# A causal convolution and a gated projection on one core: convolution units moved between the column and the row products

## The chip, the core and the metric

The kernel runs on one core of a Trainium2 chip. The core has a matrix engine (TensorE, PE in the profile, with its weight loads shown apart as PEld), three engines for elementwise work (VectorE as DVE, ScalarE as ACT, GpSimd as POOL) and SyncE (SP), which here only issues DMA transfers. Each engine takes its instructions in the order of the program; between engines, semaphores hold an instruction until its inputs are there and its output buffer is free. TensorE writes its results to PSUM, of which this kernel has eight banks of 128 x 512 fp32: two for the gate of chunk 1, one for the gate of chunk 2 and five shared by everything else.

The metric is the device time of one execution in microseconds (us), here as the median over several runs.

## The reference

x has 8 sequences of 4224 positions and 192 features, 8 heads of 24. First each head is convolved with 7 causal taps, the softmax of 7 weights. On that result x works a gated layer: a causal convolution of 5 taps for each feature gives a gate through a sigmoid, x is projected by a 192 x 192 matrix, multiplied by the gate, and projected again.

```python
w = softmax(weight)                                   # 8 heads x 7
x = einsum('hk,bskhg->bshg', w, windows(x, 7))        # causal, per head
gate_pre = sum(conv_w[k] * shifted(x, k) for k in range(5))
gate = 1 / (1 + exp(-gate_pre))
out = (gate * (x @ w_val)) @ w_out
```

## The kernel before

The features lie on the partitions and the positions along the free dimension. 192 features don't fit in 128 partitions, so two streams of four sequences each are worked together: for each position, "chunk 1" holds 128 features of both streams (a tile of 128 x 2 x m), and "chunk 2" holds the last 64 features of both streams in the halves of one tile (128 x m). In the code the index 0 or 1 of a gate stands for chunk 1 or chunk 2; in the products q = 0 and 1 are the two streams of chunk 1 and q = 2 is chunk 2. To keep the word free, the steps of the main loop are called chunks n in the text below, and "chunk-1 taps" and "chunk-2 taps" name the taps of the gate for the two tiles, whose PSUM tiles are called pa and pb in the profile.

There are 36 chunks n, of up to m = 502 positions (304 and 302 in the first two, 448 in the next six, 502 from 8 to 31, 448 to 456 and 232 in the last four). They belong to 14 groups, and each group's convolved x comes out of the first stage, as follows.

- **Convolution units** (`conv_unit`, line 312). A unit is four windows of the 7-tap convolution, each a product of a window of x (weights on PE) with a band matrix (`band`), in fp32; the profile counts two matmuls for each. The result (tile pc) is copied by ScalarE to tile e (line 321). When a head is complete, `scatter` sends it with DMAs (line 348) into x1 and x2 of the group, and `load_x` issues the next loads of x (line 160); both go through SP's queue, for the first groups partly through POOL's. There are 114 units. `conv(k)` issues the next k of them, and the list `todo` says how many belong to each chunk n: 3, 6, 3, 5, 5, 4, 3, 3 in chunks 0 to 7, then 4, 3, 3 over and over in 8 to 25, 2 each in 26 to 31, none after that. They are for a group that is needed two groups later.
- **Gates**. `gate_open` (line 382) is a ScalarE instruction that starts the gate's sum in PSUM with the first tap; `gate_taps` (line 389) adds the other four on VectorE; `gate_close` (line 402) is ScalarE's sigmoid from PSUM to SBUF (g1 and g2). pa and pb have one buffer each, so a gate is opened only after the one before it is closed, and the next taps begin only when it is open.
- **Products in split precision**. A product in fp32 is done as three products of rounded parts, high and low: `split` and `split_gated1`, `split_gated2` make the parts, the high one by a ScalarE cast (lines 410, 418), the low one by a POOL subtraction (lines 411, 419).
- **The two projections**, "v" (x times w_val, of chunk n) and "o" (the gated product times w_out, of chunk n - 1). Each has four groups on PE: `diagonal` (line 445, chunk 2 to chunk 2, full array), `main` (line 455, chunk 1 to chunk 1, full array, three matmuls for each stream), `columns` (line 483, chunk 1 to chunk 2, 64 columns of the array for each stream) and `rows` (line 468, chunk 2 to chunk 1, 64 rows of the array for each stream).
- **Ends**. `gated(n, q)` (line 502) multiplies "v" with the gate on VectorE, out of PSUM; `project(n, q)` (line 518) copies "o" out of PSUM on ScalarE, and after q = 1 the output DMA is issued on SP (line 523).

Every engine's order is that of the code (`manual_schedule`). The five shared banks (pool `ps`) go round: `pc`, "v" and "o" tiles take a bank when their first matmul comes, and give it back when their last reader is done, which is `gated` for "v", `project` for "o" and the copy of line 321 for a unit. A tile's first matmul waits for the reader that gave its bank back. The main loop stands at the end of the function.

Of the kernel before, what the change touches and what calls it, by code (L numbers as in the profile page):

```python
# [99 lines left out]
def kernel(  # L100
# [197 lines left out]
    def conv_unit(u):  # L298
        g, q, ws = units[u]
        n = NJS[g]  # L300
        if u == first_unit[g]:
            x1s[g] = xp.tile([128, 2 * XB], F32, tag="x1", name=f"x1_{g}")
            x2s[g] = xp.tile([128, XC], F32, tag="x2", name=f"x2_{g}")
        if ws[0] == (0, 0):
            es[g, q] = ep.tile([M, 4 * NMAX * WIN], F32, tag="e", name=f"e_{g}_{q}")
        e = es[g, q]
        pc = ps.tile([128, 512], F32, tag="p", name=f"pc_{u}")
        for k, (hi, j) in enumerate(ws):
            h = QUADS[q][hi]
            i, at = home[g, h]  # L310
            c = (at * n + j) * M
            nc.tensor.matmul(  # L312
                pc[:M, k * WIN : (k + 1) * WIN],
                lhsT=xtiles[i][:, c : c + M],
                rhs=band[:, 4 * q + hi, :],
                start=True,
                stop=True,
            )
        a = (ws[0][0] * n + ws[0][1]) * WIN
        w = len(ws) * WIN  # L320
        nc.scalar.copy(e[:, a : a + w], pc[:M, :w])  # L321
        done = [hi for hi, j in ws if j == n - 1]
        for hi in done:
            h = QUADS[q][hi]
            i, at = home[g, h]
            last = at == len(loads[i][1]) - 1
            if last and g >= BY_POOL:
                load_x(allowed(i))
            scatter(g, h, e[:, hi * n * WIN : (hi + 1) * n * WIN])
            if last and g < BY_POOL:  # L330
                load_x(allowed(i))
# [31 lines left out]
    def views(n, k=KG - 1):  # L363
        g, o, m = STEPS[n]
        b = second(NJS[g])
        x1v = x1s[g][:, : 2 * b].rearrange("p (a t) -> p a t", a=2)
        return x1v[:, :, o + k : o + k + m], x2s[g][:, o + k : o + k + m]
# [5 lines left out]
    def gate_open(n, i):  # L373
        if n >= N:
            return
        m = STEPS[n][2]
        if i == 0:
            acc = ps_g.tile([128, 2, 512], F32, tag="pa", name=f"pa_{n}")[:, :, :m]
        else:
            acc = ps_h.tile([128, 512], F32, tag="pb", name=f"pb_{n}")[:, :m]  # L380
        accs[n, i] = acc
        nc.scalar.mul(acc, views(n, 0)[i], cwt[:, i, 0:1])  # L382

    def gate_taps(n, i, k0=1, k1=KG):
        if n >= N:
            return
        acc = accs[n, i]
        for k in range(k0, k1):
            nc.vector.scalar_tensor_tensor(  # L389
                out=acc, in0=views(n, k)[i], scalar=cwt[:, i, k : k + 1],  # L390
                in1=acc, op0=ALU.mult, op1=ALU.add,
            )

    def gate_close(n, i):
        if n >= N:
            return
        m = STEPS[n][2]
        if i == 0:
            dst = g1s[n] = gp.tile([128, 2, MB], F32, tag="g1", name=f"g1_{n}")[:, :, :m]
        else:  # L400
            dst = g2s[n] = gp.tile([128, MB], F32, tag="g2", name=f"g2_{n}")[:, :m]
        nc.scalar.activation(dst, accs.pop((n, i)), AF.Sigmoid)  # L402
# [21 lines left out]
    def bank(what, n, q):  # L424
        t = ps.tile([128, 512], F32, tag="p", name=f"{what}_{n}_{q}")[:, : STEPS[n][2]]
        banks[what, n, q] = t
        return t

    def operands(what, n):
        return (w_val, *xs[n, 1], *xs[n, 2]) if what == "v" else (w_out, *pr[n, 1], *pr[n, 2])  # L430

    def parts(w, h, l):
        return (w.h, h), (w.l, h), (w.h, l)

    def ok(n):
        return 0 <= n < N

    def diagonal(what, n):
        if not ok(n):
            return  # L440
        acc = bank(what, n, 2)
        w, _, _, h2, l2 = operands(what, n)
        r = slice(W22, W22 + 128)
        for i, (a, b) in enumerate(parts(w, h2, l2)):
            nc.tensor.matmul(acc, lhsT=a[:, r], rhs=b, start=(i == 0), stop=False)  # L445

    def main(what, n, q):
        if not ok(n):
            return
        fresh = (what, n, q) not in banks  # L450
        acc = bank(what, n, q) if fresh else banks[what, n, q]
        w, h, l, _, _ = operands(what, n)
        r = slice(W11, W11 + 128)
        for i, (a, b) in enumerate(parts(w, h, l)):
            nc.tensor.matmul(  # L455
                acc, lhsT=a[:, r], rhs=b[:, q], start=(fresh and i == 0), stop=(not fresh and i == 2)
            )

    def rows(what, n):
        if not ok(n):  # L460
            return
        fresh = (what, n, 0) not in banks
        two = [bank(what, n, q) if fresh else banks[what, n, q] for q in range(2)]
        w, _, _, h2, l2 = operands(what, n)
        r = slice(W21, W21 + 128)
        for i, (a, b) in enumerate(parts(w, h2, l2)):
            for acc, p in zip(two, HALVES):
                nc.tensor.matmul(  # L468
                    acc, lhsT=a[p, r], rhs=b[p], start=(fresh and i == 0), stop=(not fresh and i == 2)
                )  # L470

    def columns(what, n):
        if not ok(n):
            return
        m = STEPS[n][2]
        acc = banks[what, n, 2]
        w = w_val if what == "v" else w_out
        x = views(n)[0] if what == "v" else g1s[n]
        cuts = [m * i // 4 for i in range(5)]
        for i in range(4):  # L480
            c = slice(cuts[i], cuts[i + 1])
            for q, p in enumerate(HALVES):
                nc.tensor.matmul(  # L483
                    acc[p, c], lhsT=w.f[:, W12 : W12 + 64], rhs=x[:, q, c],
                    start=False, stop=(i == 3),
                )

    def split(n):
        if n >= N:
            return  # L490
        x1, x2 = views(n)
        if n == 0:
            xs[n, 2] = split2(sp, "x", n, x2)
        xs[n, 1] = split1(sp, "x", n, x1)
        if n > 0:
            xs[n, 2] = split2(sp, "x", n, x2)

    def gated(n, q):
        if not ok(n):
            return  # L500
        v = g1s[n][:, q] if q < 2 else g2s[n]
        nc.vector.tensor_tensor(out=v, in0=banks.pop(("v", n, q)), in1=v, op=ALU.mult)  # L502

    def split_gated1(n):
        if ok(n):
            pr[n, 1] = split1(pp, "p", n, g1s[n])

    def split_gated2(n):
        if ok(n):
            pr[n, 2] = split2(pp, "p", n, g2s[n])  # L510

    def project(n, q):
        if not ok(n):
            return
        m = STEPS[n][2]
        if n not in ots:
            ots[n] = op.tile([128, 3 * MB], F32, tag="ot", name=f"ot_{n}")
        nc.scalar.copy(ots[n][:, q * m : (q + 1) * m], banks.pop(("o", n, q)))  # L518
        o = 3 * sum(s[2] for s in STEPS[:n])
        if n == LAST:  # L520
            nc.sync.dma_start(out[:, o + q * m : o + (q + 1) * m], ots[n][:, q * m : (q + 1) * m])
        elif q == 1:
            nc.sync.dma_start(out[:, o : o + 3 * m], ots[n][:, : 3 * m])
# [9 lines left out]
    def conv(k):  # L533
        for _ in range(k):
            if done[0] < len(units):
                conv_unit(done[0])
                done[0] += 1

    todo = [0] * (N + 1)
# [31 lines left out]
    for n in range(N + 1):  # L571
        diagonal("v", n)
        gate_taps(n + 1, 0, 1, 3)
        split(n + 1)
        diagonal("o", n - 1)
        main("v", n, 0)
        main("v", n, 1)
        gate_taps(n + 1, 0, 3, KG)
        columns("v", n)
        gated(n, 2)  # L580
        gate_close(n + 1, 0)
        gate_open(n + 2, 0)
        columns("o", n - 1)
        split_gated2(n)
        project(n - 1, 2)
        rows("v", n)
        gated(n, 0)
        gated(n, 1)
        rows("o", n - 1)
        split_gated1(n)  # L590
        main("o", n - 1, 0)
        gate_taps(n + 1, 1)
        project(n - 1, 0)
        main("o", n - 1, 1)
        project(n - 1, 1)
        conv(todo[n])
        gate_close(n + 1, 1)
        gate_open(n + 2, 1)

# [89 lines left out]
```

## Time and profile before

| | |
|---|---|
| median of 3 runs | 393.77 us (392.7 to 394.51) |
| the profiled execution, its own time | 391.79 us |
| its span | 390.0 us |
| its granted TensorE clock | 0.99 of full speed |
| PE, DVE, ACT, POOL busy | 377.6, 343.5, 323.7, 254.6 us |

All views come from that one profiled execution. A row of the timeline begins with its start in us from the start of the span, and its length; then follow engine, line, operation, output and inputs, shapes and count, and in brackets the idle time of the engine just before it with what ended it. Neighbouring rows of one kind are merged, so that a row of "x4" covers four instructions. Instructions of VectorE and ScalarE that follow each other overlap by a little in such rows, so the distance from start to start is less than the length. A row of the chain of waits has a start, a length and what was on the chain. In the view of waits a row names an engine with its tile and line, what it waited for, the total in us, how often and the longest. "Issue" there is idle time for which no event is seen.

### The profile page before, as it was taken

The numbers are of one execution on the slowest core, as the hardware profiler recorded it, in microseconds if no ns is written. First come the engines' busy times: TensorE is split into PE (matmuls) and PEld (weight loads), VectorE is DVE, ScalarE is ACT, GpSimd is POOL, SyncE is SP. The second block draws the span as 40 slices with busy tenths as digits, with TensorE's granted clock in tenths as the row PEclk, the third lists the DMA queues.
The fourth block names the chain that finished last, engine by engine and source line by source line (L and its number), as shares of the span: only waits on it lengthen the run. The fifth ranks groups of instructions, "written<-read, shape, count | busy, mean of one in ns | idle before, by whom it ended". The sixth has DMA issues, their size and how long they took to land.

```text
span 390.0 us, 8633 instructions
## 1 busy us (share of the span) xinstructions
PE 377.6 (97%) x3204; PEld 322.4 (83%) x3204; DVE 343.5 (88%) x432; ACT 323.7 (83%) x525; POOL 254.6 (65%) x178
## 2 busy tenths in 40 slices
PE   8778999999999999999999999999999999999895
PEld 8768989988888888888888888888888777888684
DVE  5897797888998998998999899899899999999971
ACT  5668798988888888888889888888888888887873
POOL 1968665566667665666666676666566776776781
PEclk9988999999999999999999999999999999999999
DMA  8876779998787688777767768758887644334223
GB/s 301 227 194 206 210 222 281 248 278 258 251 248 217 180 258 248 220 216 244 236 188 242 229 191 260 210 184 265 251 231 218 224 153 154 115 119 151 81 106 145
DMA packets 38226, 82.49 MB, mean 212 GB/s; under 512 B 4841, under 2 KB 17513, under 8 KB 38185
## 3 DMA queue, kind: packets, MB, share of 16 engines
q1 hardware_dynamic: 36936, 80.06, 66.7%
q0 software_dynamic: 960, 1.39, 1.5%
q8 instruction: 25, 0.41, 0.5%
q10 hardware_dynamic: 288, 0.50, 0.4%
q14 instruction: 17, 0.13, 0.1%
HBM read 29.34 MB, written 26.00 MB: 142 GB/s over the span
## 4 chain that ended last, share of the span: by engine, by line
PE 78%; DVE 11%; DMA 4%; ACT 3%; issue 2%; SPq 0%; POOL 0%; DVEq 0%; ACTq 0%
PE pc L312 22%; PE o L455 11%; PE v L455 10%; PE v L483 7%; PE v L468 6%; PE o L483 6%; PE o L468 5%; DVE pa L389 5%; PE v L445 5%; PE o L445 5%; DVE pb L389 3%; DMA x<-xw 3%; DVE g L502 2%; PE pw L204 1%; DMA x<-e 1%
## 5 line engine op out<-in xcount | busy, mean ns | idle before, releaser
L389 DVE SCALAR_TENSOR_TENSOR pa<-x,cwt,pa 128x1004 f32<-128x1004 f32 (+5 forms) x144 | 172.9, 1201 | 5.1 <-ACT pa L382 1.3
L411 POOL TENSOR_TENSOR xl<-x,xh 128x1004 fp32r<-128x1004 f32 (+5 forms) x36 | 74.7, 2075 | 75.4 <-ACT xh L410 67.8
L312 PEld LDWEIGHTS pc<-band,x 128*120 128x120 f32 x912 | 103.3, 187 | 8.4 <-DMA x<-xw 3.6
L312 PE MATMUL pc<-band,x 128*120 128x122 f32 x912 | 104.8, 272 | 5.3 <-DMA x<-xw 5.3
L389 DVE SCALAR_TENSOR_TENSOR pb<-x,cwt,pb 128x502 f32<-128x502 f32 (+5 forms) x144 | 102.3, 710 | 3.8
L502 DVE TENSOR_TENSOR g<-v,g 128x502 f32<-128x502 f32 (+5 forms) x108 | 66.0, 643 | 24.3 <-PE v L468 16.2
L411 POOL TENSOR_TENSOR pl<-g,ph 128x1004 fp32r<-128x1004 f32 (+5 forms) x36 | 79.3, 2201 | 8.3 <-ACT ph L410 6.4
L402 ACT ACTIVATE g<-pa 128x1004 f32<-128x1004 f32 (+5 forms) x36 | 34.5, 958 | 41.9 <-DVE pa L389 20.3
L419 POOL TENSOR_TENSOR pl<-g,ph 128x502 fp32r<-128x502 f32 (+5 forms) x36 | 42.9, 1191 | 37.0 <-ACT ph L418 37.0
L321 ACT COPY e<-pc 120x488 f32<-120x488 f32 x114 | 59.2, 588 | 6.1 <-PE pc L312 5.8
L518 ACT COPY ot<-o 128x502 f32<-128x502 f32 (+5 forms) x108 | 55.8, 551 | 1.2 <-PE o L455 0.7
L382 ACT ACTIVATE pa<-x,cwt 128x1004 f32<-128x1004 f32 (+5 forms) x36 | 37.8, 1050 | 6.7 <-DMA x<-e 4.9
L419 POOL TENSOR_TENSOR xl<-x,xh 128x502 fp32r<-128x502 f32 (+5 forms) x36 | 41.8, 1162 | 0.1
L483 PEld LDWEIGHTS v<-x,wvf 128*64 128x64 f32 x576 | 29.0, 136 | 11.8 <-issue 11.4
L483 PE MATMUL v<-x,wvf 128*64 128x126 f32 (+5 forms) x576 | 37.1, 270 | 0.0
L410 ACT CAST ph<-g 128x1004 fp32r<-128x1004 f32 (+5 forms) x36 | 35.1, 976 | 1.2 <-DVE g L502 1.2
L483 PE MATMUL o<-g,wof 128*64 128x126 f32 (+5 forms) x576 | 35.5, 264 | 0.0
L410 ACT CAST xh<-x 128x1004 fp32r<-128x1004 f32 (+5 forms) x36 | 34.6, 962 | 0.0
L483 PEld LDWEIGHTS o<-g,wof 128*64 128x64 f32 x576 | 30.8, 136 | 0.1
L455 PE MATMUL o<-ph,woh 128*128 128x502 f32 (+5 forms) x72 | 30.8, 428 | 0.0
L455 PE MATMUL v<-xh,wvl 128*128 128x502 f32 (+5 forms) x72 | 27.1, 376 | 0.0
L455 PE MATMUL v<-xh,wvh 128*128 128x502 f32 (+5 forms) x72 | 27.0, 376 | 0.0
(75 smaller groups left out, 574.7 us busy)
## 6 DMA issues: line engine op xcount, KB each, us to landing
x<-xw SPq DMA_DIRECT2D x64, 300.0 KB
out<-ot SPq DMA_DIRECT2D x24, 753.0 KB
x<-e SPq DMA_DIRECT2D x40, 285.9 KB
x<-xw SPq DMA_DIRECT2D x20, 360.0 KB
out<-ot SPq DMA_DIRECT2D x8, 672.0 KB
x<-e SPq DMA_DIRECT2D x32, 141.6 KB
x<-e SPq DMA_DIRECT2D x25, 171.6 KB
x<-e SPq DMA_DIRECT2D x16, 94.4 KB
```

The lines of the kernel that those rows point to most:

```text
L312: nc.tensor.matmul(pc[:M, k * WIN : (k + 1) * WIN], lhsT=xtiles[i][:, c : c + M], rhs=band[:, 4 * q + hi, :], start=True, stop=True,)
L321: nc.scalar.copy(e[:, a : a + w], pc[:M, :w])
L389: nc.vector.scalar_tensor_tensor(out=acc, in0=views(n, k)[i], scalar=cwt[:, i, k : k + 1], in1=acc, op0=ALU.mult, op1=ALU.add,)
L410: nc.scalar.copy(h, x)
L411: nc.gpsimd.tensor_tensor(out=l, in0=x, in1=h.bitcast(F32), op=ALU.subtract)
L419: nc.gpsimd.tensor_tensor(out=l, in0=x, in1=h.bitcast(F32), op=ALU.subtract)
L445: nc.tensor.matmul(acc, lhsT=a[:, r], rhs=b, start=(i == 0), stop=False)
L455: nc.tensor.matmul(acc, lhsT=a[:, r], rhs=b[:, q], start=(fresh and i == 0), stop=(not fresh and i == 2))
L468: nc.tensor.matmul(acc, lhsT=a[p, r], rhs=b[p], start=(fresh and i == 0), stop=(not fresh and i == 2))
L483: nc.tensor.matmul(acc[p, c], lhsT=w.f[:, W12 : W12 + 64], rhs=x[:, q, c], start=False, stop=(i == 3),)
L502: nc.vector.tensor_tensor(out=v, in0=banks.pop(("v", n, q)), in1=v, op=ALU.mult)
L518: nc.scalar.copy(ots[n][:, q * m : (q + 1) * m], banks.pop(("o", n, q)))
```

## The change

The body of the main loop is put in another order. The convolution units move from the end of a chunk to the place between the columns of "o" (and what follows these, `split_gated2` and `project(n - 1, 2)`) and the rows of "v". The closing of the chunk-1 gate of n + 1 and the opening of that of n + 2 stood right behind `gated(n, 2)`; they now stand behind the first and the second unit, so that ScalarE has the cast of `split_gated2`, the copy of `project` and a unit's copy ahead of the closing, and another unit's copy ahead of the opening. The chunk-2 taps of n + 1 move from behind the gated products of chunk 1 to ahead of them on VectorE. Nothing else is changed: the instructions are the same in kind, shape and number.

```diff
         columns("v", n)
         gated(n, 2)
-        gate_close(n + 1, 0)
-        gate_open(n + 2, 0)
         columns("o", n - 1)
         split_gated2(n)
         project(n - 1, 2)
+        conv(min(1, todo[n]))
+        gate_close(n + 1, 0)
+        conv(min(1, max(0, todo[n] - 1)))
+        gate_open(n + 2, 0)
+        conv(max(0, todo[n] - 2))
+        gate_taps(n + 1, 1)
         rows("v", n)
         gated(n, 0)
         gated(n, 1)
         rows("o", n - 1)
         split_gated1(n)
         main("o", n - 1, 0)
-        gate_taps(n + 1, 1)
         project(n - 1, 0)
         main("o", n - 1, 1)
         project(n - 1, 1)
-        conv(todo[n])
         gate_close(n + 1, 1)
         gate_open(n + 2, 1)
```

## The prediction

> **What bounds the kernel now.** I read the page's busy shares and its chain first, then the busy times by stage, cut where the number of convolution units per chunk changes.
>
> ```profile
> PE 377.6 (97%) x3204; PEld 322.4 (83%) x3204; DVE 343.5 (88%) x432; ACT 323.7 (83%) x525; POOL 254.6 (65%) x178
> ...
> PE 78%; DVE 11%; DMA 4%; ACT 3%; issue 2%; SPq 0%; POOL 0%; DVEq 0%; ACTq 0%
> ```
> ```profile
> 43.20:104.47 61.27, 61.27 (x559) 54.39 (x558) 52.28 (x65) 52.61 (x88) 37.84 (x24) 1.00 0.88 255
> 104.47:294.67 190.20, 190.20 (x1599) 160.94 (x1598) 175.12 (x199) 166.04 (x259) 124.25 (x73) 1.00 0.75 226
> 294.67:353.57 58.90, 58.43 (x472) 47.12 (x470) 56.77 (x66) 50.85 (x79) 40.73 (x25) 1.00 0.50 165
> 353.57:390.00 36.43, 31.05 (x282) 24.89 (x280) 25.40 (x37) 24.05 (x44) 21.96 (x15) 0.99 0.33 125
> ```
>
> Columns of the second fence: stretch and length, then busy time of PE, PEld, DVE, ACT and POOL, granted clock, DMA share and GB/s. From 43.20 to 294.67 (chunks 2 to 25) PE is busy in all of it: nothing there can be won by moving work, only by shortening PE's stream. In the 58.90 us of chunks 26 to 31, with two units each, PE waits a little and DVE, 56.77 busy, has the pace: 58.90 / 6 = 9.82 a chunk. The last stage is mixed.
>
> One chunk of the middle with three units, in the chain of waits (start, length, what):
>
> ```profile
> 154.97 2.52 PE pc L312 x24
> 157.50 0.69 PE v L445 x3
> 158.19 0.68 PE o L445 x3
> 158.87 1.37 PE v L455 x6
> 160.24 1.01 PE v L483 x16
> 161.25 0.86 PE o L483 x16
> 162.11 0.94 PE v L468 x6
> 163.05 0.70 PE o L468 x6
> 163.76 1.58 PE o L455 x6
> ```
>
> They follow each other without a gap; a unit is 2.52 / 3 = 0.84. The same number of products costs more where the group before used the array in another form: columns after the full array 1.01 against 0.86 (+0.15), rows after columns 0.94 against 0.70 (+0.24), full array after rows 1.58 against 1.37 (+0.21). Full array after full array costs nothing: 0.69 and 0.68 for "v" and "o" diagonals, the first of them behind the units. The wait view names the same three places, where the weight load was held:
>
> ```profile
> PEld o L455 <- issue: 11.7, 35, 0.4
> PEld v L483 <- issue: 11.4, 34, 0.4
> ...
> PEld v L468 <- issue: 4.0, 24, 0.2
> ```
>
> **Step 1, the units' new place on PE.** No product is added. Units (full array) now stand between columns and rows. Gone is one change of form (columns to rows); new are two (columns to full, full to rows). Neither is in this trace. Nearest rows: the first unit behaves as the full array after rows, +0.21; rows keep their 0.24. So +0.21 a chunk, with bounds of -0.24 (rows lose their surcharge, units get none) and +0.24 (units get as much as rows). It counts where PE has the pace, chunks 3 to 25: 23 x 0.21 = **+4.8** (-5.5 to +5.5).
>
> The Trainium skill, page "TensorEngine Tiling (Array Packing)", section "Key Properties", says that a change of tiling mode drains TensorE. It speaks against this change: by it, each of the two new borders costs something, and the sum is the +4.8 rather than nothing. The three surcharges above agree with it; columns to full and full to rows are in no row here.
>
> **Step 2, banks and ScalarE.** At the units the two "v" banks of the chunk are held until gated(n, 0) and (n, 1), which now come after rows. Of five banks three are left: one free from the last chunk, that of gated(n, 2), and that of project(n-1, 2). I assume that the bank freed first is taken first. ScalarE (and VectorE's wait for rows), middle:
>
> ```profile
> 156.87 1.52 ACT L321 COPY e<-pc 120x488 f32<-120x488 f32 x3
> ...
> 162.29 1.01 ACT L402 ACTIVATE g<-pa 128x1004 f32<-128x1004 f32 x1 [1.23 <-DVE pa L389]
> 163.34 1.10 ACT L382 ACTIVATE pa<-x,cwt 128x1004 f32<-128x1004 f32 x1
> 164.38 0.60 ACT L418 CAST ph<-g 128x502 fp32r<-128x502 f32 x1
> 164.88 0.57 ACT L518 COPY ot<-o 128x502 f32<-128x502 f32 x1
> ```
> ```profile
> 162.09 0.67 DVE L502 TENSOR_TENSOR g<-v,g 128x502 f32<-128x502 f32 x1
> 163.13 1.27 DVE L502 TENSOR_TENSOR g<-v,g 128x502 f32<-128x502 f32 x2 [0.37 <-PE v L468]
> ```
> ```profile
> 301.70 3.08 DVE L389 SCALAR_TENSOR_TENSOR pb<-x,cwt,pb 128x502 f32<-128x502 f32 x4
> 304.69 5.17 DVE L389 SCALAR_TENSOR_TENSOR pa<-x,cwt,pa 128x1004 f32<-128x1004 f32 x4
> 309.77 1.85 DVE L502 TENSOR_TENSOR g<-v,g 128x502 f32<-128x502 f32 x3
> ```
>
> Take the end of columns "v" as 0 (estimates, from these durations, start to start: a unit copy 0.46, its end 0.57; gate close 1.05, open 1.04). Units start at 0.86 and end, with 0.1 of the new surcharge ahead of them, at 1.80, 2.64, 3.48 (4.32 with four); rows follow and end at 4.51 (5.35). gated(n, 2) runs from about 0.32 (step 3) to 1.0, so unit 2's bank is there in time. ScalarE then has the cast, project, the copy of unit 1 from 2.01, close from 2.47, the copy of unit 2 from 3.52 to 4.09, open to 5.02, the copy of unit 3 to 5.59. Rows "o" need two banks. With three units those are unit 1's and unit 2's: 4.14 with the signal, before 4.51, no wait. With four units they are unit 2's and unit 3's, and the latter, behind the gate's opening on ScalarE, comes at 5.64 against 5.35: PE waits 0.3. Chunks 5, 8, 11, 14, 17, 20 and 23 have four: 7 x 0.3 = **+2.1** (0 to +4). Queued behind that wait are rows "o", main "o" and the next chunk's diagonals; all of PE.
>
> **Step 3, VectorE.** The chunk-2 taps (304.69 - 301.70 = 2.99) now run from 1.0 to 4.0, while PE does units and rows; the two gated products wait for rows at 4.58 and end at 5.78. Behind them the next chunk-1 taps (309.77 - 304.69 = 5.08) end at 10.86; the next columns end at 4.51 + 0.70 + 1.58 + 0.69 + 0.68 + 1.37 + 1.01 = 10.54. So the next gated(n, 2) is again 0.32 late, which is covered by unit 1: cost nothing. If that cover went, unit 2 would wait by as much as VectorE is later than about 1.1.
>
> With two units rows "o" need unit 2's bank: copy done at about 4.03 against rows' end at 3.67, a wait of 0.36, and PE's chunk becomes 10.06 against 9.82: 6 x 0.24 = +1.4. In the last stage VectorE has the pace through chunk 33:
>
> ```profile
> 357.10 1.04 PE L483 MATMUL o<-g,wof 128*64 128x125 f32 x16
> ...
> 358.52 1.70 DVE L502 TENSOR_TENSOR g<-v,g 128x448 f32<-128x448 f32 x3
> ...
> 367.60 1.68 DVE L502 TENSOR_TENSOR g<-v,g 128x448 f32<-128x448 f32 x3
> ```
>
> Its queue was about 1.2 behind columns "v" of chunk 32 (PE goes on to columns "o" at 357.10, and the gated products start at 358.52); with slower chunks before, it is less behind, and about 0.9 of the 1.4 comes back. Net **+0.5** (-1 to +2). The scatters of the last units also land 3 us earlier, which matters only to waits already inside VectorE's time.
>
> **Step 4, the start.** Units of chunk 0 wait for a load:
>
> ```profile
> 25.92 4.36 DMA x<-xw
> ...
> 30.33 2.41 PE pc L312 x12
> ...
> 36.33 0.62 PE v L468 x6
> ...
> 38.39 5.04 PE pc L312 x48
> ```
> ```profile
> 30.00 4.73 DVE L389 SCALAR_TENSOR_TENSOR pa<-x,cwt,pa 128x896 f32<-128x896 f32 x4 [0.38 <-ACT pa L382]
> ...
> 35.92 0.47 DVE L502 TENSOR_TENSOR g<-v,g 128x302 f32<-128x302 f32 x1 [1.19 <-PE v L483]
> ...
> 36.98 0.85 DVE L502 TENSOR_TENSOR g<-v,g 128x302 f32<-128x302 f32 x2 [0.59 <-PE v L468]
> ...
> 38.33 0.43 ACT L418 CAST ph<-g 128x302 fp32r<-128x302 f32 x1
> 38.66 0.40 ACT L518 COPY ot<-o 128x304 f32<-128x304 f32 x1
> ```
>
> Rows "v" of chunk 0 ran before that wait; now they stand behind it, and end at 30.33 + 2.41 + 0.7 = 33.5. Behind rows wait gated(0, 0) and (0, 1), to 34.4, and behind those on VectorE the chunk-1 taps of chunk 2, which began at 30.00: now 34.4 to 39.1, and gated(1, 2) to 39.55 instead of 36.4. In chunk 1 the units start at about 37.2; the first takes the one free bank and ends at 38.1, the second waits for gated(1, 2), to 40.4. The third waits for cast and project (0.43 + 0.40), to 41.35; the fourth runs to 42.2; the fifth, with unit 2's bank, to 43.3; the sixth waits for unit 3's copy, behind close and open, at 44.0, to 44.85. Rows and main "o" take 38.39 - 36.33 = 2.06: 46.9, where the old chunk 2 began at 43.4. That is +3.5; VectorE still late in chunk 2 adds 0.4, a wait of 0.3 in the old chunk 3 goes: **+3.6** (+0.7, rows alone, to +5). Later stages are PE's, so nothing of it comes back.
>
> SP's queue: units' scatters and loads now go ahead of the output store; SP has mostly waited for that store, so nothing is late.
>
> **Sum.** 4.8 + 2.1 + 0.5 + 3.6 = +11.0. Against the profiled execution (span 390.0, own time 391.79) that gives 402.8; the median of the runs shown is 393.77, 2.0 above it, so **404.8**.
>
> **Rivals.** (a) The new borders on PE cost no more than the old one: 404.8 - 4.8 = 400.0. For: neither border is in the trace. Against: each of the three that are there costs 0.15 to 0.24. (b) On the other side: rows lose their 0.24 behind full-array products and the units pay nothing, -5.5 over 23 chunks: 393.77 + 3.6 + 2.1 + 0.5 - 5.5 = 394.5, not slower; it decides once a chunk saves more than 6.2 / 23 = 0.27 against the old order, or a little less within the 0.5% of about 2 us, which is what a measurement of this kernel can tell from no change. (c) ScalarE's chain is later than I have it (its slack of 0.35 before rows "o" in three-unit chunks is thin), and the 14 three-unit chunks from 6 to 25 wait too, 0.5 each: 404.8 + 7.0 = 411.8. (d) VectorE, not PE, paces the middle, and the taps fill its 0.37 wait for rows, in chunks 8 to 25: 393.77 - 18 x 0.37 = 387.1. Against: PE's 190.20 of 190.20.
>
> **Chances.** Forecast 0.55, (a) 0.18, (b) 0.07, (c) 0.15, (d) 0.05. Slower by over 0.5%: forecast, (a), (c), 0.88, less a little for (a) with a small start: 0.87; (b) mostly within: 0.06; faster 0.07. The range leaves out (b), (d) and the far end of (c): 397.5 (the start alone) to 411.
>
> **What would show it.** Right: in the chain, unit groups after columns of 2.7 instead of 2.52 for three units and rows "v" still about 0.94; PE waiting for ScalarE at rows "o" in four-unit chunks; in chunk 1 PE idle at the units with VectorE's gated product as releaser, and chunk 2 starting near 47. Wrong: a three-unit chunk still of 10.3 in the middle (step 1), rows "o" at 0.70 in four-unit chunks (step 2), chunk 2 at 44 (step 4); or VectorE releasing unit 2 in every chunk, which would break step 3.

## The result and the profile after

The changed kernel takes 404.19 us (median of 6 runs, 402.01 to 405.47), the kernel before 394.08 in the same comparison (6 runs). The ratio is 1.0247, with a 95% interval of 1.0214 to 1.0279: slower, where 404.8 and slower had been predicted. Between the medians the change costs 10.1. The profiled execution took 403.16, with a span of 401.4, which is 11.4 more than in the profile of before.

The busy times and the chain of the changed kernel:

```profile
PE 385.3 (96%) x3204; PEld 323.5 (81%) x3204; DVE 343.0 (85%) x432; ACT 322.8 (80%) x525; POOL 253.5 (63%) x178
...
PE 62%; DVE 20%; ACT 7%; DMA 4%; issue 4%; POOL 1%; SPq 0%; DVEq 0%; ACTq 0%
```

No engine has more to do, as nothing was added; PE is busy for longer, 385.3 against 377.6. Its share of the chain falls from 78% to 62%: in the changed kernel the chain leaves PE at the waits for other engines that are shown below, and from chunk 26 on it runs mostly over VectorE, as it did before in chunks 26 to 31. The stages, cut where chunks 2, 8, 26 and 32 begin (the columns are those of the prediction's stages):

```profile
46.57:109.56 62.99, 62.99 (x559) 55.35 (x558) 54.44 (x67) 52.66 (x90) 38.09 (x24) 1.00 0.90 252
109.56:305.50 195.94, 195.75 (x1597) 161.81 (x1596) 175.36 (x199) 165.68 (x259) 123.54 (x72) 1.00 0.74 221
305.50:363.51 58.01, 58.01 (x469) 47.12 (x468) 56.73 (x67) 50.54 (x79) 41.18 (x24) 1.00 0.46 154
363.51:401.40 37.89, 31.29 (x280) 24.49 (x278) 24.59 (x36) 24.35 (x44) 22.27 (x15) 0.97 0.30 115
```

Against the stages of before this gives, with a chunk counted from its first "v" diagonal to the next chunk's:

| stage | before | after | difference | predicted |
|---|---|---|---|---|
| to chunk 2 | 43.20 | 46.57 | +3.4 | +3.5 |
| chunks 2 to 7 | 61.27 | 62.99 | +1.7 | chunks 2 to 25 together: +7.0 |
| chunks 8 to 25 | 190.20 | 195.94 | +5.7 | |
| chunks 26 to 31 | 58.90 | 58.01 | -0.9 | +1.4 |
| chunk 32 to the end | 36.43 | 37.89 | +1.5 | -0.9 |
| span | 390.0 | 401.4 | +11.4 | +11.0 |

One three-unit chunk of the middle, in the chain of waits (start, length, what):

```profile
153.87 0.68 PE v L445 x3
154.54 0.68 PE o L445 x3
155.22 1.36 PE v L455 x6
156.58 1.02 PE v L483 x16
157.60 0.86 PE o L483 x16
158.46 2.71 PE pc L312 x24
161.17 0.88 PE v L468 x6
162.05 0.68 PE o L468 x6
162.73 1.55 PE o L455 x6
```

The units take 2.71 instead of 2.52 now that they follow the columns. Rows "v", behind the units instead of behind the columns, take 0.88 against rows "o" of 0.68; in the kernel before they took 0.94 in one chunk and 0.88 in the next, against 0.70, so they kept their surcharge. So each chunk pays for four changes of the array's form instead of three: three-unit chunks of 8 to 25 take 10.45 on average against 10.31, which is +0.14.

A four-unit chunk has in addition a wait at rows "o". First PE and ScalarE in the timeline, then the wait view:

```profile
183.59 0.93 PE L468 MATMUL o<-ph,woh 64*128 64x502 f32 x2
```
```profile
182.34 1.14 ACT L382 ACTIVATE pa<-x,cwt 128x1004 f32<-128x1004 f32 x1
183.38 1.06 ACT L321 COPY e<-pc 120x488 f32<-120x488 f32 x2
```
```profile
PEld o L468 <- ACT e L321: 3.0, 7, 0.5
```

The two first matmuls of rows "o" go to two banks and normally run side by side (0.39 for the pair in a three-unit chunk). Here the second waits for the copy of the third unit, which ScalarE begins at 183.38, behind the gate's opening. It happens 7 times, in the seven chunks with four units; those of 11 to 23 take 11.82 against 11.14.

The start, with PE and VectorE in the timeline:

```profile
31.53 1.52 PE L312 MATMUL pc<-band,x 128*120 128x122 f32 x12 [2.37 <-DMA x<-xw]
...
33.70 0.85 DVE L502 TENSOR_TENSOR g<-v,g 128x304 f32<-128x304 f32 x2 [3.24 <-PE v L468]
...
34.47 4.72 DVE L389 SCALAR_TENSOR_TENSOR pa<-x,cwt,pa 128x896 f32<-128x896 f32 x4
...
39.10 0.47 DVE L502 TENSOR_TENSOR g<-v,g 128x302 f32<-128x302 f32 x1
...
39.62 3.63 PE L312 MATMUL pc<-band,x 128*120 128x122 f32 x32 [1.83 <-DVE g L502]
...
43.56 1.10 PE L312 MATMUL pc<-band,x 128*120 128x122 f32 x8 [0.31 <-ACT e L321]
```

The rows of chunk 0 stand behind the units that wait for a load; VectorE waits 3.24 for them, then has the gated products and four taps to do, and only then the gated product for whose bank the second unit of chunk 1 waits 1.83 on PE. The sixth unit waits for a copy. Those are the links of step 4. The load itself landed 1.2 later than in the profile of before (31.53 against 30.33). On the other hand the 12 unit matmuls behind it took 1.52 instead of 2.41: in the profile of before the granted clock was 0.50 from 30.77 to 34.18, in this one it was 1.00 from 27.36 on. So the +3.4 of this one pair of profiles isn't a clean measure.

### The profile page after: what moved, and what is told of

It is laid out like the page before. It is cut to its first block, busy times and chain, and to the rows that moved or that the text cites. A ratio compares the mean times of both kernels' runs of the same rounds, so it can differ in the third digit from the quotient of the medians.

```text
span 401.4 us, 8600 instructions
## 1 busy us (share of the span) xinstructions
PE 385.3 (96%) x3204; PEld 323.5 (81%) x3204; DVE 343.0 (85%) x432; ACT 322.8 (80%) x525; POOL 253.5 (63%) x178
## 4 chain that ended last, share of the span: by engine, by line
PE 62%; DVE 20%; ACT 7%; DMA 4%; issue 4%; POOL 1%; SPq 0%; DVEq 0%; ACTq 0%
PE pc L312 18%; DVE pa L389 10%; PE o L455 9%; PE v L455 8%; PE v L483 6%; DVE g L502 6%; PE v L468 5%; PE o L483 5%; PE o L468 5%; DVE pb L389 4%; PE o L445 4%; PE v L445 4%; DMA x<-e 2%; ACT e L321 2%; ACT pa L382 1%
## 5 line engine op out<-in xcount | busy, mean ns | idle before, releaser
L312 PE MATMUL pc<-band,x 128*120 128x122 f32 x912 | 108.4, 275 | 8.1 <-DMA x<-xw 5.6
L312 PEld LDWEIGHTS pc<-band,x 128*120 128x120 f32 x912 | 100.6, 186 | 14.9 <-issue 6.2
L321 ACT COPY e<-pc 120x488 f32<-120x488 f32 x114 | 64.1, 580 | 5.1 <-PE pc L312 5.0
L418 ACT CAST ph<-g 128x502 fp32r<-128x502 f32 (+5 forms) x36 | 21.1, 585 | 39.0 <-DVE g L502 39.0
L382 ACT ACTIVATE pa<-x,cwt 128x1004 f32<-128x1004 f32 (+5 forms) x36 | 38.8, 1078 | 3.0 <-DMA x<-e 2.9
```

What stands on the lines that cost most here:

```text
L312: nc.tensor.matmul(pc[:M, k * WIN : (k + 1) * WIN], lhsT=xtiles[i][:, c : c + M], rhs=band[:, 4 * q + hi, :], start=True, stop=True,)
```

## The experiments

Chunk lengths below are from the profile of each run; times are medians beside the kernel before in the same comparison. The changed kernel itself was measured in another comparison than these runs, and the median of the kernel before went from 392.99 to 394.08 between comparisons, so a difference of about 1 us from the changed kernel says little.

**The gate opened behind all units.**

```diff
         conv(min(1, max(0, todo[n] - 1)))
-        gate_open(n + 2, 0)
         conv(max(0, todo[n] - 2))
+        gate_open(n + 2, 0)
```

> The changed kernel with the chunk-1 gate opened behind all units of the chunk instead of behind the second. My theory (in four-unit chunks rows "o" wait 0.53 for the third unit's copy, which ScalarE does behind the opening): these waits go, 7 x 0.53 = 3.7, four-unit chunks 11.3 instead of 11.81; the opening ends 0.5 to 0.9 later, about when VectorE is ready for it, so little is given back: 400.5. Rival (the wait is for the gated products or the array): four-unit chunks stay 11.8 and the time 404; or the later opening delays the taps by 0.5 a chunk in all chunks: 404 + 12 = 416.

400.13 against 393.74, ratio 1.0174 (1.0153 to 1.0195): 4.1 below the changed kernel, or 3.7 when each is taken against its own kernel before. ScalarE and PE in a four-unit chunk:

```profile
180.76 1.58 ACT L321 COPY e<-pc 120x488 f32<-120x488 f32 x3
182.25 1.11 ACT L382 ACTIVATE pa<-x,cwt 128x1004 f32<-128x1004 f32 x1
```
```profile
182.46 0.39 PE L468 MATMUL o<-ph,woh 64*128 64x502 f32 x2
182.69 0.39 PE L468 MATMUL o<-ph,wol 64*128 64x502 f32 x2
```

The copies are done before the opening, and rows "o" run as pairs without a wait. Chunk 14 takes 11.27 instead of 11.83, and the seven four-unit chunks together 3.5 less. Three-unit chunks of 8 to 25 stay at 10.42 to 10.49, but for chunk 9, which takes 10.88 instead of 10.45: there the units wait a little for ScalarE. So the bank wait is ScalarE's order of copies and opening, and the later opening gives back no more than that one chunk.

**Two more form changes in the kernel before.**

```diff
-        diagonal("o", n - 1)
         main("v", n, 0)
...
+        diagonal("o", n - 1)
         columns("o", n - 1)
```

> The kernel before with the diagonal of "o" moved between the columns of "v" and those of "o": PE's products are the same, but each chunk has one step from columns to full array and one from full array to columns more. My theory (a change of the array's form costs 0.15 to 0.21): 0.34 a chunk more in the 24 chunks in which PE has the pace, 8 us: 402, three-unit chunks 10.65 instead of 10.31. Rival (such steps cost nothing, and what the changed kernel loses in the middle is something else): 394, chunks 10.31.

402.67 against 393.74, ratio 1.0227 (1.0210 to 1.0245). The chain of a three-unit chunk:

```profile
164.37 1.01 PE v L483 x16
165.38 0.89 PE o L445 x3
166.27 1.01 PE o L483 x16
167.29 0.91 PE v L468 x4
...
170.44 2.52 PE pc L312 x24
```

The diagonal of "o" costs 0.89 behind columns, where it cost 0.68 behind the full array, and the columns of "o" 1.01 where they cost 0.86 behind those of "v". The units, back behind main "o", have their 2.52. Three-unit chunks take 10.60 to 10.67, on average +0.32 against 10.31. The price of a form change is shown in a kernel in which nothing else of the change is made.

**The taps alone, in the kernel before.**

```diff
+        gate_taps(n + 1, 1)
         rows("v", n)
...
         main("o", n - 1, 0)
-        gate_taps(n + 1, 1)
```

> The kernel before with one part of the change: the chunk-2 taps ahead of the two gated products, units and gates in the old places. My theory (PE has the pace; the gated products come 2.7 later and the first unit, which takes a bank of theirs, waits about 0.34 for it at 4.42 against 4.08 after the columns): 24 chunks x 0.34 = 8, and the last stage 1.5 longer because project stands behind a cast that waits for the gated products: 402 to 403. Rival (VectorE has the pace and the taps fill its waits before the gated products): 394.1 - 18 x 0.37 = 387.

406.24 against 393.74, ratio 1.0322 (1.0303 to 1.0340), and three-unit chunks of 10.70. Without the units between them the taps hold the gated products back. VectorE's timeline and the wait view:

```profile
169.06 3.08 DVE L389 SCALAR_TENSOR_TENSOR pb<-x,cwt,pb 128x502 f32<-128x502 f32 x4
172.05 1.26 DVE L502 TENSOR_TENSOR g<-v,g 128x502 f32<-128x502 f32 x2
```
```profile
PEld pc L312 <- ACT ot L518: 19.5, 31, 1.5
```

The gated products start right behind the taps, at 172.05, when rows "v" have long ended (169.12 to 170.10 in PE's timeline). PE then waits before the units. The wait view names project's copy as the last releaser, not the gated product that I had expected, and the copy is no later than before: it begins 3.54 behind the end of columns "v" (171.86 against 168.32), where it was 3.63 before (164.88 against 161.25). So what the taps hold back is the gated products; that the first unit had taken a bank of theirs before, and now gets project's since theirs come later still, fits the rows but is not shown by them. The middle went as expected (+0.39 a chunk against 0.34), the total was 3 to 4 worse than expected; chunk 32, for one, took 9.48 against 7.98. That VectorE paces the middle and the taps would fill its waits, which would have given 387, is refuted.

**The taps back, the units in their new place.**

```diff
-        gate_taps(n + 1, 1)
         rows("v", n)
...
         main("o", n - 1, 0)
+        gate_taps(n + 1, 1)
```

> The changed kernel with the chunk-2 taps behind the gated products, as before the change; units and gates stay in their new places. My theory (the taps ahead are what VectorE does while PE works on the units; without them it idles there and VectorE's round becomes the bound: gated product 0.65, wait for units 2 and 3 and rows, gated products 1.2, eight taps 8.07 = 12.8 a three-unit chunk against 10.46): chunks 2 to 31 longer by about 2.2 each, 404 + 66 = 470, PE waiting for the second unit's bank from VectorE. Rival (PE stays the bound): 404 to 406.

504.49 in one run, against 393.42. The wait view, PE's timeline and the granted clock of the run:

```profile
PEld pc L312 <- DVE g L502: 71.2, 31, 4.2
```
```profile
200.17 2.71 PE L312 MATMUL pc<-band,x 128*120 128x122 f32 x16 [2.22 <-DVE g L502]
...
202.82 0.79 PE L468 MATMUL v<-xh,wvh 64*128 64x502 f32 x2
...
203.40 0.62 PE L468 MATMUL v<-xh,wvl 64*128 64x502 f32 x2
```
```profile
core 0: 502.7 us, clock 0.932
```

PE waits 31 times for the second unit's bank, 1.4 to 4.0 us each, as expected, and VectorE's round is the bound: this is what the taps' new place covers. The size was underestimated by a third (+100 against +66). Behind the wait shown PE runs slower: 16 unit matmuls take 2.71 where 24 do elsewhere, and a pair of rows 0.79 and 0.62 against 0.49 and 0.39. The granted clock (the third number from the end of a row of the view by stretches) tells why:

```profile
201.74:205.16 3.42, 3.42 (x19) 2.69 (x17) 0.62 (x2) 2.83 (x4) 0.35 (x1) 0.50 0.50 133
205.16:229.05 23.89, 19.92 (x158) 16.01 (x155) 18.81 (x22) 15.21 (x24) 13.14 (x8) 1.00 0.55 172
```

It is 0.50 for 3.4 us and then 1.00 again; behind the next wait, at full clock, 16 unit matmuls take 2.22 and the pairs of rows 0.50 and 0.40. The mean over the run is 0.932 against 0.989 in the changed kernel. In chunks 8 to 31 the six three-unit chunks without such a stretch take 12.95 on average, close to the 12.8 of my theory, and the six with one take 14.53. So VectorE's round was sized rightly for three units; what was missing in the sum are the clock and the larger loss of four-unit chunks (14.77 without a stretch against 11.82, where 2.2 more was expected).

**The start: three runs.** Chunk 0 alone in the old order of its units (in the changed kernel), then chunks 0 and 1 wholly in the old order, then chunk 0 alone in the new order in the kernel before.

```diff
-        conv(min(1, todo[n]))
+        if n > 0:
+            conv(min(1, todo[n]))
...
         project(n - 1, 1)
+        if n == 0:
+            conv(todo[n])
```

> The changed kernel with chunk 0 alone in the old order of its units (at its end); chunks 1 and later as changed. My theory (rows of chunk 0 behind the load, then gated products, taps and the second unit's bank in chunk 1 lost 3.4 us by the start of chunk 2): 404.2 - 3.4 + about 0.3 for chunk 1, whose sixth unit still waits for a copy = 401.1, chunk 2 starting near 43.5. Rival (the start was later only because the load itself landed later): 404, chunk 2 again near 46.

402.02 against 393.74, ratio 1.0215 (1.0194 to 1.0237): 2.2 below the changed kernel's median (1.8 when each is taken against its own kernel before), less than expected. In its profile chunk 2 begins at 46.10, as the rival said; but the loads landed later still (total wait, times, longest; the changed kernel had 5.6 in all):

```profile
PE pc L312 <- DMA x<-xw: 8.2, 2, 4.2
```

The load on which chunk 0's units wait landed at 32.77 here. From that landing to the start of chunk 2 it is 13.3 us. In the profiles of the kernel before and of the runs below with chunks 0 and 1 in the old order it is 12.9 to 13.7, in those of the changed kernel and of the two runs that keep its start, or nearly (the gate opened last, the old taps at the end) 15.0 to 16.8. Counted so, the new start costs 1.3 to 3.9, chunk 0 has all of it or nearly all, and the rival falls.

> The changed kernel with chunks 0 and 1 wholly in the old order (units, gates and taps); chunks 2 and later as changed. With chunk 0 alone in the old order the time was 402.02, 2.2 below the changed kernel's, and chunk 1 still took 11.74 against 10.80 before. My theory: the start costs about 3.1 in all, of which chunk 1 holds the other 0.9: 401.1, with chunk 1 back at about 10.8 when its loads land in time. Rival (chunk 0 was all of it, the rest of chunk 1's length is the loads' landing, which differs from run to run): 402.0.

401.57 against 393.42, ratio 1.0205 (1.0159 to 1.0250). Chunk 1 took 11.21, chunk 2 began at 44.69, but chunk 2 then took 10.26 against 9.01 in the changed kernel. The interval holds both sides' numbers, so the time doesn't decide; counted from the load's landing (31.02) the start took 13.7, no less than with chunk 0 alone, which speaks for the rival.

```diff
+        if n == 0:
+            conv(1)
+            gate_close(n + 1, 0)
+            conv(1)
+            gate_open(n + 2, 0)
+            conv(todo[n] - 2)
+            gate_taps(n + 1, 1)
         rows("v", n)
...
```

> The kernel before with chunk 0 alone in the changed order (units ahead of rows, gates between the units, taps ahead of the gated products). My theory (rows of chunk 0 wait behind the units for the load, and the gated products, the taps of chunk 2 and the gated product of chunk 1 come some 3 us later; in the old order of chunk 1, rows "o" wait for that gated product's bank): 393.6 + 2.5 to 3.5 = 396.5, with PE released by VectorE in chunk 1 near 39.7. Rival (chunk 0's order is worth nothing by itself, what the start lost is the loads' landing): 393.6.

397.66 against 392.99, ratio 1.0110 (1.0087 to 1.0132), which is 3.4 to 5.2 us for chunk 0 alone. VectorE and PE:

```profile
35.51 0.86 DVE L502 TENSOR_TENSOR g<-v,g 128x304 f32<-128x304 f32 x2 [6.18 <-PE v L468]
...
40.91 1.22 DVE L502 TENSOR_TENSOR g<-v,g 128x302 f32<-128x302 f32 x3
```
```profile
41.43 0.41 PE L468 MATMUL o<-ph,woh 64*128 64x304 f32 x1 [2.12 <-DVE g L502]
```

VectorE waits 6.18 for the rows behind the units, and PE later waits 2.12 for VectorE's gated product. The mechanism is shown, and its price in the old kernel, which holds some lower clock: it was 0.50 from 28.37 to 35.20 and from 42.03 to 45.44 in this profile. What exactly it costs in the new one lies between 1 and 4 by these runs, since the loads' landing varies by as much.

**The taps of the last chunks.**

```diff
-        gate_taps(n + 1, 1)
+        if n < 32:
+            gate_taps(n + 1, 1)
         rows("v", n)
...
         main("o", n - 1, 0)
+        if n >= 32:
+            gate_taps(n + 1, 1)
```

> The changed kernel with the chunk-2 taps behind the gated products again in chunks 32 and later, which have no units. My theory (in the last stage VectorE is late, the taps ahead delay the gated products of chunk 1, project stands behind the cast that waits for them, and PE waits for project's bank: chunks 34 and 35 of 8.4 and longer against 7.25): 1.2 to 1.5 less: 402.8, chunk 34 at 7.3. Rival (VectorE's sum of work sets the end, whatever its order): 404.2.

404.35 against 393.42, ratio 1.0267 (1.0235 to 1.0299): nothing gained. In the changed kernel PE's wait in the last stage is for project (first fence, its wait view from 363 on); with the old order it is for VectorE (second fence, the wait view from 360 on, and third, VectorE's timeline):

```profile
PEld v L455 <- ACT ot L518: 2.2, 3, 0.9
```
```profile
PEld o L468 <- DVE g L502: 2.3, 1, 2.3
```
```profile
374.43 4.79 DVE L389 SCALAR_TENSOR_TENSOR pa<-x,cwt,pa 128x912 f32<-128x912 f32 x4
379.13 1.68 DVE L502 TENSOR_TENSOR g<-v,g 128x448 f32<-128x448 f32 x3
```

One wait took the place of the other: chunk 34 did not go to 7.3 (8.28), and chunk 33 grew to 9.68 from 8.65. My theory of the end fell, and the rival's number came out. That VectorE's sum of work sets the end whatever its order is more than the runs show: behind PE's wait for VectorE the granted clock was 0.50 from 381.57 to 384.99, which the changed kernel's profile doesn't have there and which lies mostly in chunk 34, and with the taps alone moved in the old kernel this stage took 39.1 against 36.4.

**All mends at once.** Chunks 0 and 1 in the old order, the opening behind all units, the old taps in chunks 32 and later (the edits above together).

> All three mends at once: chunks 0 and 1 in the old order, the opening behind all units, the old taps in chunks 32 and later. My theory: what is left is the one more change of the array's form, 0.14 a chunk in 24 chunks = 3.4, and nothing else: 394.0 + 3.4 = 397.4, three-unit chunks still 10.45, four-unit chunks 11.3. Rival (the three losses overlap, or there is one that I haven't named): 399 or more. If the form change cost nothing: 394.

399.20 against 393.42, ratio 1.0140 (1.0101 to 1.0179): better than the changed kernel, still slower than the one before. From chunk 10 on three-unit chunks take 10.42 to 10.49 (one of them 10.68), four-unit chunks 11.26 to 11.32, as expected. The total lies 1.8 above my number, on the rival's side. Stage by stage the profile is longer than that of before by 0.8 up to chunk 2, 2.4 in chunks 2 to 7, 2.9 in 8 to 25 and 1.1 from 32 on, and shorter by 0.9 in 26 to 31. The form change thus explains the middle, not the rest. Part of that is in chunk 2 (10.23 in its profile), where the units, now earlier, wait for loads on PE:

```profile
48.21 1.49 PE L312 MATMUL pc<-band,x 128*120 128x122 f32 x12 [0.21 <-DMA x<-xw]
50.65 1.52 PE L312 MATMUL pc<-band,x 128*120 128x122 f32 x12 [0.95 <-DMA x<-xw]
```

**The units between rows "o" and main "o".** Gates and taps as in the kernel before.

```diff
         split_gated1(n)
+        conv(todo[n])
         main("o", n - 1, 0)
...
         project(n - 1, 1)
-        conv(todo[n])
         gate_close(n + 1, 1)
```

> The kernel before with the units one place earlier, between rows "o" and main "o"; gates and taps as before. PE changes form three times a chunk as in the kernel before (rows to full array at the units instead of at main "o"), and no bank of "v" is held over the units. My theory (what the change lost in the middle is the fourth form change and the bank wait, not the earlier place): three-unit chunks 10.3 to 10.4, total 394 to 395. Rival (any earlier place of the units costs, since gated products or casts then come later): 398 or more, chunks 10.45.

401.81 against 392.99, ratio 1.0212 (1.0184 to 1.0239). A miss: chunks 12 and 13 take 10.47 and 10.57 (three-unit chunks +0.19 on average), chunk 11 takes 11.81. There are three form changes here as before, but the first unit now comes before a "v" bank is free. VectorE, PE and the wait view:

```profile
158.04 1.27 DVE L502 TENSOR_TENSOR g<-v,g 128x502 f32<-128x502 f32 x2 [1.02 <-PE v L468]
...
158.78 2.78 PE L312 MATMUL pc<-band,x 128*120 128x122 f32 x24 [0.16 <-DVE g L502]
```
```profile
PEld pc L312 <- DVE g L502: 16.5, 31, 0.6
```

So another place of the units isn't free even without a fourth form change: each place has its own bank to wait for. In the kernel before, main "o" stood between the gated products and the units and covered that wait. In chunk 11 the fourth unit waits for a unit's copy on ScalarE besides. My expectation had looked at forms and not at the banks of the new place.

## Why the prediction was right, step by step

**What bounds the kernel.** Right. PE had the pace in chunks 2 to 25, and the loss there is 7.5 of the 11.4 in the profiles.

**Step 1, the form change.** Right in mechanism, too large in size: +0.21 a chunk was taken, +0.14 measured. The units' surcharge is 0.19 (2.71 against 2.52), close to the 0.21 taken from main behind rows, and rows "v" kept theirs. What was missed is on the other side: counted from start to start, the "v" diagonal takes 0.76 behind the units in the kernel before and 0.68 now that main "o" is ahead of it, so the old place of the units had a small price too, which the prediction put at nothing. Over the 23 chunks it is 3.2 instead of 4.8. The experiment with the diagonal shows the price of columns to full (0.21) and of full to columns (0.15) by itself. The rivals with no cost, or a gain, at the borders fell.

**Step 2, the banks.** Right in mechanism for four units, too small in size: 0.3 was taken; a four-unit chunk grew by 0.68, of which 0.14 is the form change and 0.54 the wait. ScalarE's copy came when it was expected (begun at 183.38, 4.92 behind the columns "v" ending at 178.46; the prediction had 5.02). But the prediction counted the wait from the end of rows "v", 5.35 (measured 183.76 - 178.46 = 5.30), while rows "o" stood ready at 5.13, as neighbouring matmuls overlap by about 0.2 in the view. Opening the gate last took 3.7 to 4.1 us off the time and 3.5 off the seven chunks, against 7 x 0.54 = 3.8. Three-unit chunks don't wait, as predicted, so the third rival fell too.

With two units this step was wrong. I had rows "o" wait for the second unit's bank. In the order that I had assumed, which the four-unit chunks bear out, two units leave project's bank and the first unit's for rows "o", and both are free in time: no wait of PE there, and chunks 26 to 31 took 9.67 instead of 10.06. That is even less than the 9.82 of before. The chain of waits runs over VectorE in these chunks in both kernels; its work is the same (56.77 and 56.73), and its idle time fell from 2.1 to 1.3: before, 0.8 of it was a wait for rows "v", which is gone now that the taps stand ahead.

**Step 3, VectorE.** Right that the taps ahead cost nothing in the middle and that the units cover them: without that order the time is 504. For the end I had a loss of 1.4 in chunks 26 to 31 and 0.9 coming back behind them; it was 0.9 won and then 1.5 lost. That the net +0.6 is close to the predicted +0.5 is luck: both parts had the wrong sign. In the last stage PE waits for project's copy in three places (2.2 in its weight loads); with the old taps there it waits as long for VectorE instead, so what sets the end stays open.

**Step 4, the start.** Right: the links in the profile are those predicted. That gated(1, 2) comes at 39.10 where 39.1 had been the end of the taps is partly luck, as the load came 1.2 later and the units behind it, at full clock, took 0.9 less. For its size there are +3.4 in the profiles, 1.8 to 2.2 when chunk 0 is put back, 1.3 to 3.9 counted from the load's landing, and 3.4 to 5.2 when chunk 0 alone is changed in the old kernel. The predicted 3.6 is among them, in the upper part; no closer value is settled. The rival that it was only the loads falls with the run on the old kernel and with the counts from the landing.

**The sum.** 404.8 against 404.19, or +11.0 against +10.1 between the medians. The parts were less exact than the sum, and that it came so close is in part luck: step 1 was 1.6 too large, step 2 some 1.7 too small.

## What to carry to other kernels

Where one engine streams without a gap, look first at what an order adds to that stream: here the same products cost 0.15 to 0.24 us more behind a change of the array's form. Then, for every product moved, ask which PSUM bank it will take, who gives that bank back and what stands ahead of that reader on its engine; two of the edits tried here (the taps alone, the units behind rows) failed on that question. And where another engine has the pace, as VectorE has in the last chunks here, a wait that is removed from the first engine can come back under another name.

## What the runs showed of the hardware that I had not expected

Going from columns to rows costs rows "v" 0.18 to 0.24 (0.88 and 0.94 against 0.70) and going from the full array to rows about 0.20 (0.88 against 0.68); the full array costs 0.21 behind rows and 0.19 to 0.21 behind columns. So in these rows the surcharge shows in the group that begins and depends little on the form before it. The Trainium skill, page "TensorEngine Tiling (Array Packing)", section "Key Properties", says that a change of the tiling mode drains TensorE; these rows agree with it.

Units and columns work in fp32, the other groups in its rounded form, so some of these borders change the type as well. The type isn't the cause: rows to main "o" (0.21) and columns to units (0.19) change the form alone. Main "o" to units and units to the "v" diagonal change the type alone, and there the units have no fixed part (2.52 for three, 3.36 for four) and the diagonal takes 0.69 against 0.68, or 0.08 more when counted from start to start.

With the taps back the expected 470 became 504, at a mean granted clock of 0.932. Between 7 us and the end the trace has the clock at 1.00 but for stretches of 3.4 us (one of 6.8) at 0.50, and 16 of the 30 chunks from 2 to 31 hold one. From the means of the chunks with and without one, those of 8 to 31 lost about 18 us to it (an estimate: 6 x 1.58 with three units, 4 x 0.55 with four, 4 x 1.57 with two). All the waits for VectorE behind chunk 1 are of 1.4 to 2.7 us there, and the runs don't tell which of them is followed by such a stretch: one of 2.22 that ends at 200.17 is, one of 2.21 that ends at 243.35 isn't.
